# An LSH attention and mixing kernel: a new instruction order, scaling chains in single steps, another bias instruction, and fp32 weights for four heads

## The chip, the cores and the metric

The kernel runs on one core of a Trainium2 chip. The core has four compute engines with a queue of instructions each: PE (TensorE, matmuls; PEld is its weight loads), DVE (VectorE), ACT (ScalarE) and POOL (GpSimd). A fifth queue, SP, issues the DMAs. Each engine works its own queue strictly in order, and waits for other engines by semaphores. The metric is the time of one execution on the device in microseconds (us).

## The reference

Four batches of eight heads, 768 tokens, 64 dimensions a head. Tokens whose six projection signs agree share a bucket and may attend to one another; the heads' outputs, joined to 512 columns, go through a mixing block.

```python
mask = q_bucket[:, :, :, None] == k_bucket[:, :, None, :]
scores = np.where(mask, scale * np.matmul(q, k.transpose(0, 1, 3, 2)), -1e9)
attn = np.exp(scores - np.max(scores, axis=-1, keepdims=True))
attn = attn / (np.sum(attn, axis=-1, keepdims=True) + 1e-09)
x = join_heads(np.matmul(attn, v))
theta = x @ w_theta
y = w_tok_r @ (x * cos(theta)) + w_tok_i @ (x * sin(theta))
u = x + y
out = u + np.maximum(u @ w_ch, 0.0)
```

All inputs are fp32. The kernel reaches that precision with fp16 matmuls on pairs of tiles, a rounded part and the remainder.

## The kernel before

**Staging.** Each operand of a matmul is split into an fp16 high part and an fp16 remainder. The scale for that comes from a sum of squares and a short run of instructions on single columns (128x1): `root_scale` (four of them, for v and for two weight matrices), `pow2_scale` (three, for the six slabs of the token weights) and the seven in `prep_qk` for a pair of heads. In the kernel before each such run is one planned step, so that its instructions stand together in DVE's queue.

**Attention.** For one head, scores come in six chunks of 128x768 in PSUM (`st`). ACT takes the exponential into an fp32 tile `pf`; step p1 (DVE or ACT) rounds it into the first half of an fp16 tile `pp`; step p2 (POOL or DVE) writes the remainder `pf - pp` into the second half; then 18 matmuls, three terms for six blocks, accumulate into `po`. Twenty heads take their row maxima from a second set of scores (`sq`, DVE reduces them into `mx`). Twelve heads of batches 1 to 3 (`turned`, those of TURNED) take the maximum of the chunk itself: DVE reduces PSUM into a column of `bm`, two instructions on that column make a rate and a bias, ACT's exponential waits for both, and `pp` is turned by a DMA into `late` before its matmuls.

**Mixing.** For each batch `moe` makes theta (`ps_th`), `rest` and `mag`, sine and cosine, products `f`, their fp16 parts `z`, the token mix `py` (36 matmuls of 512 columns for 128 rows), and the channel mix `ps_r`. Batch b's mixing lies beside batch b+1's attention; that of the last batch stands alone at the end.

**What sets the order.** A table of text, ORDER, names each step and its engine in one long sequence; `issue_all` walks it and issues each step on the engine named. A second table, SLOTS, gives each step its buffer number. So ORDER decides p1, p2 and the other movable steps' engine and each queue's order; semaphores decide the time. The sequence was made by a planner outside the kernel, which the kernel doesn't hold; the durations in `on(...)` are its figures.

**The switch for single heads.** FULL lists pairs (pair of heads, head in it) of batch 0 that skip p1 and p2: they feed `pf` in fp32 as weights against an fp32 tile `vw` of v. It is empty in the kernel before.

Of the kernel before, what the change touches and what calls it, by code (L numbers as in the profile page):

```python
# [32 lines left out]
def lsh_attention_moe_kernel(ctx: ExitStack, tc: tile.TileContext, q, k, v, proj, w_theta, w_tok_r, w_tok_i, w_ch, aff, out):  # L33
# [133 lines left out]
    sinv, wsum, tinv, tsc = (const.tile([P, T], F32, name=nm) for nm in ("sinv", "wsum", "tinv", "tsc"))  # L167
# [6 lines left out]
    def pow2_scale(amax, inv, s):  # L174
        DVE.tensor_scalar(inv, amax, 1e-30, 2.0**-13, ALU.max, ALU.mult)
        DVE.tensor_scalar(inv.bitcast(U32), inv.bitcast(U32), MASK, None, ALU.bitwise_and)
        DVE.tensor_scalar(s.bitcast(U32), inv.bitcast(U32), MASK, None, ALU.bitwise_xor)

    def root_scale(total, r, inv):
        DVE.tensor_scalar(r, total, 1e-30, None, ALU.max)  # L180
        DVE.tensor_scalar(r.bitcast(U32), r.bitcast(U32), 24, 23, ALU.logical_shift_right, ALU.logical_shift_left)
        DVE.tensor_scalar(inv, r, 2.0**66, None, ALU.mult)
        DVE.tensor_scalar(r.bitcast(U32), inv.bitcast(U32), MASK, None, ALU.bitwise_xor)

    def widened(srcs, n, nm, tag, prio, am=None, stage="x", by=1.0, scaled=None, into=None, hold=()):
# [32 lines left out]
        if scaled:  # L218
            h_ = op("wscale", prio, on("DVE", 440, lambda: scaled(t)), [t["abs"]])
# [10 lines left out]
    def prep_weight(src, dst, nm, n, tag, stage, prio, step, by=1.0):  # L230
# [18 lines left out]
        def joined():  # L249
            DVE.tensor_reduce(col, sums, AX.X, ALU.add)  # L250
            DVE.tensor_scalar(col, col, 2.0**-14, col, ALU.mult, ALU.mult)
            DVE.tensor_scalar(col, col, 2.0**-14, None, ALU.mult)
# [6 lines left out]
        a = op("wcol", last_, on("DVE", 450, joined), done)  # L259
        a = op("wall", last_, on("PE", 60, total), [a], [sa])  # L260
        r = op("wcsc", last_, on("DVE", 620, lambda: root_scale(u["pa"], csc[nm], cinv[nm])), [a], [sa])
# [57 lines left out]
    def prep_v(b, hp, prio):  # L319
# [35 lines left out]
        def scale():  # L355
            root_scale(t["pa"], sc, vinv[:, col])
# [52 lines left out]
        r = op("vscale", prio, on("DVE", 630, scale), [r], [sa])  # L409
# [30 lines left out]
    def prep_qk(b, hp, G, g):  # L440
# [45 lines left out]
        def scale():  # L486
            c = t["sc"]
            sq_, sk_ = c[:, 2:3], c[:, 3:4]
            DVE.tensor_scalar(sk_, t["pa"][:, 0:1], 1e-30, None, ALU.max)
            DVE.reciprocal(sk_, sk_)  # L490
            DVE.tensor_scalar(sq_, t["pa"][:, 1:2], 1e-30, sk_, ALU.max, ALU.mult)
            DVE.tensor_scalar(sq_.bitcast(U32), sq_.bitcast(U32), 24, 23, ALU.logical_shift_right, ALU.logical_shift_left)
            DVE.tensor_scalar(sq_, sq_, 2.0**64 * math.sqrt(UNIT), None, ALU.mult)
            DVE.tensor_scalar(sk_.bitcast(U32), sq_.bitcast(U32), MASK, None, ALU.bitwise_xor)
            DVE.tensor_scalar(sk_, sk_, UNIT / 2, None, ALU.mult)
# [264 lines left out]
    def turned(g, b, h, n_, asm, vt, pieces):  # L760
# [5 lines left out]
        for i in range(T):  # L766
            def one(i=i, before=done[-1:]):
# [22 lines left out]
                def bias():  # L790
                    DVE.scalar_tensor_tensor(part(2), part(0), math.log(PSC) / CEXP, part(1), ALU.add, ALU.mult)  # L791
# [295 lines left out]
FULL = []  # L1087
# [52 lines left out]
D5n D91 A5t P66 P68 D67 D69 A99 A62 P64 S2 D65 P9a P6c D6d P6a D6b P6e D6f A1x P6g A92 S7i S7h P7n A94 P7j D95 A5 D6h S6j D6i D93 D7k P96  # L1140
D7o Scb P6l A1y D9b P6q D3 A6m D6n P7r A6r A9c P6v G6o D7s D63 A6w P70 S6k A71 Scd P7p Pcl D97 S9h P7l S9i A6x G6y P6p D9d D7q D7m Acc P7t
D7u A6s P75 G6t P7v D1z D7w Ace S7y A76 Pcf D7x P7a S7z P9n Dcg P6u A7b A72 A7c D9o P9p D9q P6z A77 P9j G73 Acj D9k P9r D9s Ach Dck P9e P85
# [12 lines left out]
Ahl Ghm Si7 A22 P1l Pju Djv Ajl D33 A35 D23 Pi9 Aia Phd Sl7 D34 Pk4 Si8 Aib Phi Dk5 Dmr Pie Pk0 A36 Gic Aif A1m Pij Phn Dk1 Aig Djm G37 S38
Pjw Dho Gih Djx Aik Ail Amu Pid Dim Pio Dmv D1n Gjn Pit Aip Aiq Pk6 D39 Dk7 Aiu Gjo Dhp Pii Aiv Giw Pin Piy P27 A3b D3a Aiz Sl8 Plf Sk9 Pjp
# [136 lines left out]
```

## Time and profile before

| | before |
|---|---|
| median of three runs | 798.91 us (797.78 to 803.15) |
| the profiled execution | 801.53 us, span of its instructions 799.8 us |
| PE busy | 683.9 us, 86% |
| DVE busy | 690.1 us, 86% |
| ACT busy | 498.6 us, 62% |
| POOL busy | 377.5 us, 47% |

An engine is counted busy while one of its instructions is shown as running. That includes time in which an instruction has started and is held up inside, so a busy share is no measure of work done.

### The profile page before, as it was taken

To read this page: it belongs to the slowest core of one execution; us is meant where nothing else is said; L and a number is where in the kernel's file an instruction comes from. 1 tells how busy PE (TensorE), PEld (TensorE's weight loads), DVE (VectorE), ACT (ScalarE), POOL (GpSimd) and SP (SyncE) were. 2 spreads that over 40 slices of the span, in tenths; PEclk is the share of its full clock that TensorE was granted. 3 is DMA by queue.
4 is the path that set the end of the run, shared out by engine and by line. 5 is a ranking of instruction groups with operands and counts; after the bars stand their busy time and mean duration, and the time that the engine had idled before them with its cause. 6 is when DMAs were issued, how large, how long until landed. Compare 5 with 4: busy or idle time off the path is not lost.

```text
span 799.8 us, 16615 instructions
## 1 busy us (share of the span) xinstructions
PE 683.9 (86%) x6372; PEld 389.3 (49%) x6372; DVE 690.1 (86%) x1210; ACT 498.6 (62%) x702; POOL 377.5 (47%) x258
## 2 busy tenths in 40 slices
PE   3877877878779889898798998899989988979997
PEld 1355655544434455555453564455535454534443
DVE  7979999999999999899999989889998868978412
ACT  6867987976676566766765567548865455545011
POOL 3266767853576544575454445363435234223101
PEclk9988999989999999999989999999999999989999
DMA  6435444433358566697544965996347744862114
GB/s 238 139 91 148 127 131 136 118 127 97 70 141 168 128 136 155 137 165 175 118 85 103 174 129 125 153 203 156 80 113 132 115 97 83 146 124 66 27 40 118
DMA packets 198415, 100.31 MB, mean 125 GB/s; under 512 B 170608, under 2 KB 188096, under 8 KB 198336
## 3 DMA queue, kind: packets, MB, share of 16 engines
q1 hardware_dynamic: 198336, 99.26, 55.6%
q8 instruction: 50, 0.82, 0.4%
q14 instruction: 29, 0.24, 0.1%
HBM read 32.51 MB, written 6.29 MB: 49 GB/s over the span
## 4 chain that ended last, share of the span: by engine, by line
DVE 45%; PE 26%; DMA 9%; ACT 7%; issue 7%; POOL 3%; SPq 2%; DVEq 0%; ACTq 0%; POOLq 0%
PE py L82 8%; DVE mx L610 5%; PE st L82 5%; DVE bm L785 4%; PE po L82 4%; DVE f L974 4%; DVE pp L668 3%; PE ps_r L82 3%; DVE hl L470 3%; DVE bm L791 3%; DMA late<-pp 2%; DVE pp L672 2%; DMA w_t<-in_moe_w_tok_i_dram 2%; PE ps_th L82 2%; POOL pp L672 2%
## 5 line engine op out<-in xcount | busy, mean ns | idle before, releaser
L672 POOL TENSOR_TENSOR pp<-pf,pp 128x768 f16<-128x768 f32 x154 | 280.6, 1831 | 273.0 <-DVE pp L668 115.8
L82 PE MATMUL py<-z,wtk 128*128 128x512 f16 x864 | 210.3, 386 | 11.6 <-POOL z L985 4.8
L655 ACT ACTIVATE pf<-st 128x768 f32<-128x768 f32 x120 | 95.7, 805 | 67.4 <-PE st L82 45.0
L82 PEld LDWEIGHTS <-wtk 128*128 128x128 f16 x864 | 83.9, 99 | 107.4 <-issue 22.7
L610 DVE TENSOR_REDUCE mx<-sq 128x1 f32<-128x768 f32 x120 | 111.9, 948 | 15.3 <-PE sq L82 14.9
L666 ACT ACTIVATE pp<-pf 128x768 f16<-128x768 f32 x131 | 108.9, 838 | 24.5 <-DMA late<-pp 12.6
L657 ACT ACTIVATE pf<-st,bm 128x768 f32<-128x768 f32 x72 | 70.7, 987 | 68.0 <-DVE bm L791 49.2
L82 PE MATMUL st<-qt,kt 108*128 108x384 f16 x480 | 100.7, 337 | 9.7 <-ACT pf L655 3.9
L82 PEld LDWEIGHTS <-pp 128*128 128x128 f16 x2160 | 86.4, 100 | 35.3 <-issue 9.5
L82 PE MATMUL po<-vv,pp 128*128 128x65 f16 (+1 forms) x2160 | 93.3, 197 | 11.6 <-DVE pp L672 5.9
L82 PEld LDWEIGHTS <-qt 108*128 108x128 f16 (+1 forms) x528 | 50.3, 102 | 81.1 <-issue 52.8
L985 POOL TENSOR_TENSOR z<-f,z 128x512 f16<-128x512 f32 x36 | 48.3, 1347 | 86.3 <-ACT z L979 47.0
L82 PE MATMUL sq<-kt,qt 108*128 108x384 f16 x240 | 62.6, 351 | 21.2 <-ACT pf L655 6.9
L82 PE MATMUL ps_th<-wth,t_x 128*128 128x512 f16 x288 | 71.0, 397 | 8.7 <-DMA t_x<-s_x 6.6
L785 DVE TENSOR_REDUCE bm<-st 128x1 f32<-128x768 f32 x72 | 67.8, 947 | 8.3 <-PE st L82 8.3
L82 PE MATMUL st<-kt,qt 108*128 108x384 f16 (+1 forms) x288 | 60.6, 335 | 16.1 <-ACT pf L657 15.1
L82 PE MATMUL ps_r<-wch,t_u 128*128 128x512 f16 x288 | 70.3, 384 | 1.0 <-DMA t_u<-s_u 0.9
L82 PEld LDWEIGHTS <-kt 108*128 108x128 f16 x480 | 45.3, 101 | 44.8 <-issue 21.5
L82 PEld LDWEIGHTS <-late 128*128 128x128 f16 x1296 | 48.1, 99 | 14.6 <-issue 2.8
L82 PE MATMUL po<-vv,late 128*128 128x65 f16 x1296 | 50.3, 195 | 4.5 <-DMA late<-pp 1.9
L668 DVE CAST pp<-pf 128x768 f16<-128x768 f32 x61 | 42.9, 705 | 9.2 <-DMA late<-pp 5.1
L82 PEld LDWEIGHTS <-t_x 128*128 128x128 f16 x288 | 28.2, 102 | 42.9 <-issue 8.3
(166 smaller groups left out, 995.3 us busy)
## 6 DMA issues: line engine op xcount, KB each, us to landing
raw<-in_q_dram SPq DMA_DIRECT2D x16, 384.0 KB
raw<-in_k_dram SPq DMA_DIRECT2D x16, 384.0 KB
vb<-in_v_dram SPq DMA_DIRECT2D x16, 384.0 KB
out_dram<-x SPq DMA_DIRECT2D x24, 256.0 KB
qt<-hl SPq DMA_DIRECT2D x31, 192.0 KB
kt<-hl SPq DMA_DIRECT2D x31, 192.0 KB
w_t<-in_moe_w_tok_r_dram SPq DMA_DIRECT2D x6, 768.0 KB
w_t<-in_moe_w_tok_i_dram SPq DMA_DIRECT2D x6, 768.0 KB
```

The lines of the kernel that those rows point to most:

```text
L82: PE.matmul(out_, l, r, start=start, stop=stop, skip_group_check=True)
L470: DVE.scalar_tensor_tensor(t["hl"][:, 1, i], t["raw", i], t["sc"][:, 2 + i : 3 + i], t["hl"][:, 0, i], ALU.mult, ALU.subtract)
L610: DVE.tensor_reduce(col()[:, i : i + 1], u["sq"], AX.XY, ALU.max)
L655: ACT.activation(u["f"], u["w"], AF.Exp, scale=CEXP)
L657: ACT.activation(u["f"], u["w"], AF.Exp, bias=bias(), scale=scale())
L666: ACT.activation(u["p"][:, 0], flat(), AF.Copy)
L668: DVE.tensor_copy(u["p"][:, 0], flat())
L672: return lambda: eng.tensor_tensor(u["p"][:, 1], flat(), u["p"][:, 0], ALU.subtract)
L785: DVE.tensor_reduce(part(0), u["w"], AX.XY, ALU.max, negate=True)
L791: DVE.scalar_tensor_tensor(part(2), part(0), math.log(PSC) / CEXP, part(1), ALU.add, ALU.mult)
L974: DVE.scalar_tensor_tensor(u["f"], tl[b][:, tt], zsc[:, b : b + 1], t["zw"][r][:, tt], ALU.mult, ALU.mult)
L985: return lambda: eng.tensor_tensor(t["z"][r, 1][:, tt], u["f"], t["z"][r, 0][:, tt], ALU.subtract)
```

## The change

1. **A new ORDER and new SLOTS.** All of both tables. In the new sequence GpSimd's steps and those VectorE steps whose operands lie in SBUF are laid out in turns. Steps also change engine.
2. **Chains.** `root_scale`, `pow2_scale`, the seven instructions of `prep_qk` and three of `prep_weight` become lists; a new `chain` makes each instruction a step of its own, so that ORDER can put other instructions between them.
3. **Bias.** The second column instruction of a turned chunk is `tensor_scalar` where it was `scalar_tensor_tensor`, with the same numbers.
4. **Four heads in fp32.** FULL holds the second head of each pair of batch 0: 24 chunks lose p1, p2 and 18 fp16 matmuls each and gain six fp32 matmuls each.

```diff
+    def chain(name, prio, fns, deps=(), slots=()):
+        r = list(deps)
+        for f in fns:
+            r = [op(name, prio, on("DVE", 75, f), r, slots)]
+        return r[0]
...
     def root_scale(total, r, inv):
-        DVE.tensor_scalar(r, total, 1e-30, None, ALU.max)
-        DVE.tensor_scalar(r.bitcast(U32), r.bitcast(U32), 24, 23, ALU.logical_shift_right, ALU.logical_shift_left)
-        DVE.tensor_scalar(inv, r, 2.0**66, None, ALU.mult)
-        DVE.tensor_scalar(r.bitcast(U32), inv.bitcast(U32), MASK, None, ALU.bitwise_xor)
+        return [
+            lambda: DVE.tensor_scalar(r, total(), 1e-30, None, ALU.max),
...
-        r = op("qksc", pr, on("DVE", 1260, scale), [r], [sa, ssc])
+        r = chain("qksc", pr, scale, [r], [sa, ssc])
...
                 def bias():
-                    DVE.scalar_tensor_tensor(part(2), part(0), math.log(PSC) / CEXP, part(1), ALU.add, ALU.mult)
+                    DVE.tensor_scalar(part(2), part(0), math.log(PSC) / CEXP, part(1), ALU.add, ALU.mult)
...
-FULL = []
+FULL = [(0, 1), (1, 1), (2, 1), (3, 1)]
...
-S5c A5d S5e A5f P5g S0 D1 P5m D5h S5v A5w D5o P5x S1u D5y A5k D5l A5i D5j S8w A5z D60 A5u S8y A5r P61 S98 D1v A5q D5s A8x A8z P90 A5p D1w
+S60 A61 S5y A5z P62 S0 D1 P6e S6n D63 D64 D65 D66 D67 D6g D68 A6o P6p D6q D69 A6a S22 D6f A6c D6d S8d D6r D6b S9h D6s A25 D6i D6k D6h D6l
```

Instructions of the built programs, where their numbers differ:

| instruction | before | after |
|---|---|---|
| PE, fp16 matmuls po from `pp` | 2160 | 1728 |
| PE, fp32 matmuls po from `pf` and `vw` | 0 | 144 |
| PE, fp32 matmuls pm from `vw` | 0 | 24 |
| DVE, casts of `pf` (p1) | 61 | 38 |
| ACT, casts of `pf` (p1) | 131 | 130 |
| POOL, remainders of `pf` (p2) | 154 | 129 |
| DVE, remainders of `pf` (p2) | 38 | 39 |
| POOL, remainders `z` | 36 | 18 |
| DVE, remainders `z` | 12 | 30 |
| DVE, casts to `z` | 27 | 17 |
| ACT, casts to `z` | 21 | 31 |
| DVE, casts of `x` and `u` (`s_x`, `s_u`) | 23 | 18 |
| ACT, casts of `x` and `u` | 25 | 30 |
| POOL, final sums of `x` | 15 | 18 |

DVE's queue, the run of seven for the third pair of heads of batch 1 (`sc_1_2`), before the change; `f` and `z` are products and parts of batch 0's mixing:

```order
L974 SCALAR_TENSOR_TENSOR f_0_1_0_3016<-x_0_656,zsc_111,z1_0_2569 128x512
L981 CAST z1_0_2569<-f_0_0_1_3014 128x512
L489 TENSOR_SCALAR sc_1_2_2780<-pq_1_2_3020 128x1
L490 RECIPROCAL sc_1_2_2780<-sc_1_2_2780 128x1
L491 TENSOR_SCALAR sc_1_2_2780<-pq_1_2_3020,sc_1_2_2780 128x1
L492 TENSOR_SCALAR sc_1_2_2780<-sc_1_2_2780 128x1
L493 TENSOR_SCALAR sc_1_2_2780<-sc_1_2_2780 128x1
L494 TENSOR_SCALAR sc_1_2_2780<-sc_1_2_2780 128x1
L495 TENSOR_SCALAR sc_1_2_2780<-sc_1_2_2780 128x1
L940 SCALAR_TENSOR_TENSOR z1_0_2569<-n_0_4_3055,mg_0_2562,ps_th0_4_2956 128x512
```

The same run in DVE's queue of the change; `bm` are the rate (L803) and bias (L806) of a turned head, `sinv` and `scw` the run of three of a token slab:

```order
L504 RECIPROCAL sc_1_2_2426<-sc_1_2_2426 128x1
L505 TENSOR_SCALAR sc_1_2_2426<-pq_1_2_2749,sc_1_2_2426 128x1
L803 TENSOR_SCALAR bm_1_2_1_2754<-bm_1_2_1_2754 128x1
L182 TENSOR_SCALAR sinv_100<-wsum_101 128x1
L506 TENSOR_SCALAR sc_1_2_2426<-sc_1_2_2426 128x1
L507 TENSOR_SCALAR sc_1_2_2426<-sc_1_2_2426 128x1
L806 TENSOR_SCALAR bm_1_2_1_2754<-bm_1_2_1_2754 128x1
L1000 TENSOR_TENSOR z1_0_2267<-f_0_2_1_2720,z1_0_2267 128x512
L183 TENSOR_SCALAR sinv_100<-sinv_100 128x1
L803 TENSOR_SCALAR bm_1_2_1_2754<-bm_1_2_1_2754 128x1
L806 TENSOR_SCALAR bm_1_2_1_2754<-bm_1_2_1_2754 128x1
L184 TENSOR_SCALAR scw_104<-sinv_100 128x1
```

Three runs now lie in one another, and the bias has become a TENSOR_SCALAR. Over the whole of DVE's queue an instruction of these runs and of the others stands right behind the one whose result it reads 384 times before and 309 times now.

PE's queue at the second chunk of head 1 of batch 0 (`po_0_1_0`), before the change, the first six of 36 rows:

```order
L82 LDWEIGHTS pp_0_1_1_580
L82 MATMUL po_0_1_0_680<-vv0_112,pp_0_1_1_580 128x65
L82 LDWEIGHTS pp_0_1_1_580
L82 MATMUL po_0_1_0_680<-vv0_112,pp_0_1_1_580 128x64
L82 LDWEIGHTS pp_0_1_1_580
L82 MATMUL po_0_1_0_680<-vv0_112,pp_0_1_1_580 128x65
```

The same chunk in PE's queue of the change, with what stands around it (`st` are scores, `pmx` turned row maxima):

```order
L82 LDWEIGHTS kt1_137
L82 MATMUL st_0_1_2_625<-qt1_134,kt1_137 128x384
L82 MATMUL po_0_1_0_605<-vw0_129,pf_0_1_1_578 128x65 x6
L635 MATMUL pmx_0_2_639<-ident_75,mx_0_2_451 6x128
L82 LDWEIGHTS kt1_137
```

Six fp32 matmuls, which load their own weights, stand where 18 pairs stood.

## Rows read from the trace of the kernel before

**Rows 1.** The page: busy us, share of the span and instructions of each engine
```profile
PE 683.9 (86%) x6372; PEld 389.3 (49%) x6372; DVE 690.1 (86%) x1210; ACT 498.6 (62%) x702; POOL 377.5 (47%) x258
```

**Rows 2.** Windows: us, then each engine's busy us and instructions, PEclk, DMA
```profile
50.00:250.00 200.00, 158.84 (x1753) 100.14 (x1752) 191.12 (x309) 157.20 (x236) 133.75 (x74) 0.95 0.45 124
250.00:700.00 450.00, 407.79 (x3962) 234.05 (x3960) 410.82 (x741) 280.13 (x384) 207.05 (x139) 0.97 0.67 133
700.00:800.00 100.00, 86.76 (x479) 40.06 (x477) 48.77 (x77) 27.06 (x36) 19.47 (x14) 0.97 0.32 75
300.00:350.00 50.00, 46.91 (x483) 27.62 (x480) 46.91 (x89) 33.56 (x46) 26.31 (x16) 0.98 0.75 150
```

**Rows 3.** Timeline, DVE, around 400 us: start us, length us, instruction
```profile
400.33 0.15 DVE L788 TENSOR_SCALAR bm<-bm 128x1 f32<-128x1 f32 x1
400.40 0.19 DVE L686 RECIPROCAL rc<-po 128x6 f32<-128x6 f32 x1
400.52 1.58 DVE L791 SCALAR_TENSOR_TENSOR bm<-bm 128x1 f32<-128x1 f32 x1
```

**Rows 4.** Single lines: count, shortest/median/longest ns, first and last start us
```profile
L791 DVE SCALAR_TENSOR_TENSOR bm<-bm x72: 118/160/1644, 222.6 to 702.7; 128x1 f32<-128x1 f32 x72
L788 DVE TENSOR_SCALAR bm<-bm x72: 111/153/155, 221.2 to 702.5; 128x1 f32<-128x1 f32 x72
L859 DVE TENSOR_SCALAR qu<-tinv,zinv,cinv_ch x4: 276/282/1615, 306.5 to 765.4; 128x6 f32<-128x6 f32 x4
L672 POOL TENSOR_TENSOR pp<-pf,pp x154: 1632/1646/4746, 33.3 to 701.4; 128x768 f16<-128x768 f32 x154
L470 DVE SCALAR_TENSOR_TENSOR hl<-raw,sc,hl x32: 996/1012/2481, 11.4 to 645.6; 128x768 f16<-128x768 f32 x32
L974 DVE SCALAR_TENSOR_TENSOR f<-x,zsc,z x48: 735/744/2207, 206.2 to 742.0; 128x512 f32<-128x512 f32 x48
L668 DVE CAST pp<-pf x61: 537/554/1998, 32.6 to 704.2; 128x768 f16<-128x768 f32 x61
L672 DVE TENSOR_TENSOR pp<-pf,pp x38: 939/952/2276, 129.8 to 705.3; 128x768 f16<-128x768 f32 x38
```

**Rows 5.** Groups: line, instruction, count | busy us, mean ns of one | idle before
```profile
L791 DVE SCALAR_TENSOR_TENSOR bm<-bm 128x1 f32<-128x1 f32 x72 | 34.2, 475 | 1.7
L470 DVE SCALAR_TENSOR_TENSOR hl<-raw,sc,hl 128x768 f16<-128x768 f32 x32 | 44.4, 1394 | 0.0
L974 DVE SCALAR_TENSOR_TENSOR f<-x,zsc,z 128x512 f32<-128x512 f32 x48 | 46.6, 986 | 2.0 <-ACT z L963 1.8
L668 DVE CAST pp<-pf 128x768 f16<-128x768 f32 x61 | 42.9, 705 | 9.2 <-DMA late<-pp 5.1 <-ACT pf L657 1.9 <-PE po L82 1.3
L672 DVE TENSOR_TENSOR pp<-pf,pp 128x768 f16<-128x768 f32 x38 | 44.4, 1170 | 3.0 <-ACT pp L666 2.7
```

**Rows 6.** The same view: groups that other terms of the sum use
```profile
L849 DVE TENSOR_SCALAR sw<-sinv,zinv 128x1 f32<-128x1 f32 x6 | 1.2, 200 | 0.0
L985 DVE TENSOR_TENSOR z<-f,z 128x512 f16<-128x512 f32 x12 | 9.8, 825 | 0.1
L981 DVE CAST z<-f 128x512 f16<-128x512 f32 x27 | 14.8, 552 | 0.5
L82 PE MATMUL pa<-vs,ones 128*128 128x1 f32 x32 | 5.6, 243 | 1.2 <-DMA kt<-rows 1.2
```

**Rows 7.** Timeline around 500 us: a run of four for v on DVE
```profile
500.35 0.15 DVE L181 TENSOR_SCALAR vsc<-vsc 128x1 uint32<-128x1 uint32 x1
500.54 0.15 DVE L182 TENSOR_SCALAR vinv<-vsc 128x1 f32<-128x1 f32 x1
```

**Rows 8.** Timeline, PE: an fp16 chunk of po and what follows; four fp32 transposes
```profile
210.44 0.72 PE L82 MATMUL po<-vv,pp 128*128 128x65 f16 x18
211.00 0.33 PE L82 MATMUL st<-qt,kt 108*128 108x384 f16 x1
...
68.71 0.68 PE L290 MATMUL pwt<-ident,wf_t 128*128 128x128 f32 x4
```

More of the change, by code (lines that the diff above doesn't have):

```diff
@@ L166, in lsh_attention_moe_kernel @@
     wtk = {(r, i): wtk_[i][:, r] for r in range(2) for i in range(2)}
-    sinv, wsum, tinv, tsc = (const.tile([P, T], F32, name=nm) for nm in ("sinv", "wsum", "tinv", "tsc"))
+    sinv, wsum, tinv, tsc, scw = (const.tile([P, T], F32, name=nm) for nm in ("sinv", "wsum", "tinv", "tsc", "scw"))
     cinv, csc = {}, {}
@@ L218, in widened @@
         if scaled:
-            h_ = op("wscale", prio, on("DVE", 440, lambda: scaled(t)), [t["abs"]])
+            h_ = chain("wscale", prio, scaled(t), [t["abs"]])
             g = op("wmul", prio, on("DVE", 60 + 535 * k_, lambda: DVE.scalar_tensor_tensor(t["f"], t["f"], t["s"], t["sg"], ALU.mult, ALU.mult)), [d, h_], [sz])
@@ L247, in prep_weight @@
                 done.append(g)
[L249 to L252, printed above, removed]
+        joined = [
+            lambda: DVE.tensor_reduce(col, sums, AX.X, ALU.add),
+            lambda: DVE.tensor_scalar(col, col, 2.0**-14, col, ALU.mult, ALU.mult),
+            lambda: DVE.tensor_scalar(col, col, 2.0**-14, None, ALU.mult),
+        ]
         def total():
@@ L258, in prep_weight @@
         last_ = prio + step * (NC * DM // n - 1)
-        a = op("wcol", last_, on("DVE", 450, joined), done)
+        a = chain("wcol", last_, joined, done)
         a = op("wall", last_, on("PE", 60, total), [a], [sa])
-        r = op("wcsc", last_, on("DVE", 620, lambda: root_scale(u["pa"], csc[nm], cinv[nm])), [a], [sa])
+        r = chain("wcsc", last_, root_scale(lambda: u["pa"], csc[nm], cinv[nm]), [a], [sa])
         for c in range(NC):
@@ L408, in prep_v @@
         r = op("vall", prio, on("PE", 60, total), [r], [svb, sa])
-        r = op("vscale", prio, on("DVE", 630, scale), [r], [sa])
+        r = chain("vscale", prio, scale, [r], [sa])
         vready[b].append(r)
@@ L484, in total, with fq, fk @@
             mm(t["pa"], ones, t["sc"][:, :2], True, True)
[L486 to L495, printed above, removed]
+        def fq():
+            return t["sc"][:, 2:3]
+        def fk():
+            return t["sc"][:, 3:4]
+        scale = [
+            lambda: DVE.tensor_scalar(fk(), t["pa"][:, 0:1], 1e-30, None, ALU.max),
+            lambda: DVE.reciprocal(fk(), fk()),
+            lambda: DVE.tensor_scalar(fq(), t["pa"][:, 1:2], 1e-30, fk(), ALU.max, ALU.mult),
+            lambda: DVE.tensor_scalar(fq().bitcast(U32), fq().bitcast(U32), 24, 23, ALU.logical_shift_right, ALU.logical_shift_left),
+            lambda: DVE.tensor_scalar(fq(), fq(), 2.0**64 * math.sqrt(UNIT), None, ALU.mult),
+            lambda: DVE.tensor_scalar(fk().bitcast(U32), fq().bitcast(U32), MASK, None, ALU.bitwise_xor),
+            lambda: DVE.tensor_scalar(fk(), fk(), UNIT / 2, None, ALU.mult),
+        ]
         r = op("qksum", pr, on("PE", 60, total), sq, [sa, ssc])
-        r = op("qksc", pr, on("DVE", 1260, scale), [r], [sa, ssc])
+        r = chain("qksc", pr, scale, [r], [sa, ssc])
         for i, sn, high, low in parts:
@@ L1137 @@
+    "001111000121130021012020221101310101100020100300110201121"
 )
 ORDER = """
[L1139 to L1142 removed]
@@ L1245 @@
+P2kt A2ku D2kv S2kw
 """
```

251 lines of the change are left out of this document (131 added, 120 removed).

## Prediction

> **What bounds the kernel now.** I read the page's busy times first: DVE and PE are level, 690.1 and 683.9 us of a span of 799.8 [rows 1]. The windows say where each leads. From 50 to 250 us DVE is busy 191.1 of 200 us and PE 158.8; from 250 to 700 us they are level, 410.8 and 407.8 of 450; the last 100 us are the last batch's mixing, PE 86.8 and DVE 48.8 [rows 2]. So DVE leads at first, then both do, then PE.
>
> Then I asked what DVE's busy time is made of. One turned chunk around 400 us shows it [rows 3]: the rate, on one column, takes 0.15 us, and the bias on the same column 1.58. A one-column instruction has no work for 1.58 us; it has started and is held. Over all 72 it takes 160 ns in the median and up to 1644, and GpSimd's remainder takes 1646 in the median [rows 4]: the longest hold is one whole GpSimd instruction. The rate, a TENSOR_SCALAR on the same column, never takes over 155 [rows 4]. Other VectorE work with its operands in SBUF shows the same pair, a short median and a longest about one GpSimd instruction above it: 1012 and 2481 ns for `hl`, 744 and 2207 for `f`, 554 and 1998 for casts of `pf` [rows 4]. So the two engines take turns on something that these forms need.
>
> Mean less median, times the count, is the time held [rows 4, 5]: bias (475 - 160) x 72 = 22.7 us; `hl` (1394 - 1012) x 32 = 12.2; `f` (986 - 744) x 48 = 11.6; casts (705 - 554) x 61 = 9.2; DVE's remainders (1170 - 952) x 38 = 8.3. That is 64.0 us of DVE's 690.1, in five groups alone.
>
> **The bias.** Its nearest row is L849, a TENSOR_SCALAR on one column with a second column as operand: 200 ns in the mean of six [rows 6]. L788, on one column too, speaks for no hold; L859, on six columns with two more operands, for one, 1615 at the longest [rows 4]. Bounds: nothing gained, and 72 x (475 - 153) = 23.2 us. I take L849's mean, since width and kind agree: 72 x (475 - 200) = 19.8 us.
>
> The Trainium skill, "SBUF — State Buffer", section "Who interferes with whom", says that a VectorE instruction with two SBUF inputs shuts out a GpSimd instruction that reads SBUF, and the reverse, and that a `tensor_scalar` can as well, in a mode that uses both ports. The trace agrees on the first (1644 ns against 160). Were the second true of one column, the bias would gain nothing, which is rival 2; rows L788 and L849 speak against it here.
>
> **The turns.** The other four groups are held 41.3 us. How much the new order removes no row shows. From the table itself: behind 78 of GpSimd's 226 entries the next VectorE entry of the old sequence is of a kind held above, and behind 35 of 187 in the new one, a share of 0.35 against 0.19. I let the hold shrink as the counts, 78 to 35, so by 55%: 22.7 us. Bounds: nothing, if the holds only move, and 41.3.
>
> **Moved work on DVE.** Casts of `pf`: 23 fewer at 0.705 = -16.2 us; remainders `z`: 18 more at 0.825 = +14.9; casts to `z`: 10 fewer at 0.552 = -5.5 [rows 5, 6]. One remainder of `pf` more and eight smaller steps handed away about cancel. Net -7 us. ACT takes 15 of the casts, and with 498.6 us busy it has room [rows 1].
>
> **The chains.** A column instruction that reads the one before it starts 0.19 us after it, with a length of 0.15 [rows 7]. One that doesn't starts 0.07 after it (L686 behind L788) [rows 3]. So a neighbour put between saves up to 0.11, and there are 75 fewer such pairs in DVE's queue: 8.3 us. Bounds: nothing and 8.3.
>
> The Trainium skill, "VectorE: DVE Perf Modes", section "The DRAIN you can't avoid", holds that the next operation doesn't start until the pipe is empty, so that only the count of operations matters. By it the chains gain nothing. The trace differs: 400.40 lies inside the 0.15 us that began at 400.33.
>
> **DVE's sum.** 19.8 + 22.7 + 7 + 8.3 = 57.8 us less, 690.1 to 632.3. What covers this gain is PE.
>
> **PE.** An fp16 chunk of 18 pairs takes 0.56 us until the next tile's matmul starts [rows 8]; 24 of them go, 13.4 us. An fp32 matmul leaves two records (the 16 calls for v's sum of squares show 32) [rows 6]. The trace has no fp32 matmul with 128 weight columns and many streamed. Nearest are the transposes, 128x128 fp32: four take 0.68 us [rows 8]; less a last one of about 0.3, which is an estimate from their common length in that row and the 243 ns of the smallest fp32 ones [rows 6], three steps are 0.38, so 0.127 a record. 144 x 2 x 0.127 = 36.6 us. Net +23.2 us, so PE goes to 707. Bounds: records as cheap as fp16 ones (0.56 / 18 = 0.031) give 9.0 - 13.4 = -4.4; records at 0.68 / 4 = 0.17 give 49.0 - 13.4 = +35.6. The 24 for the mean of v are left at nothing: an estimate of 24 x 2 x 0.127 less half of what 48 fp16 ones cost now is under 4 us, and PE is not waited for where they stand, in the first pairs' preparation; without that cover they cost those 4 us.
>
> GpSimd loses 25 remainders and 18 of `z` and so some 55 of its 377.5 us; it bounded nothing, but each of its instructions that goes is one fewer that holds DVE (already in the turns). The fp32 chunks also wait for the exponential alone, no longer for p1 and p2. I price that at nothing: it is cover for PE.
>
> **To time.** I spread DVE's gain over 50 to 700 us, 0.089 us for each. All of PE's cost falls in batch 0, before 250.
> - 50 to 250: DVE 191.1 - 17.8 = 173.3; at its present share of 0.956 that takes 181.3 us. PE 158.8 + 23.2 = 182.0, which doesn't fit. PE becomes the limit. Its best 50 us now are 46.9 of 50, 0.938, with DVE at 46.9 too [rows 2]. With DVE eased I take 0.95: 191.6 us, a gain of 8.4.
> - 250 to 700: DVE 410.8 - 40.0 = 370.8; at its present 0.913 that is 406 us. PE 407.8 / 0.95 = 429.3. A gain of 20.7.
> - the last 100 us: nothing. PE leads there and none of its work goes.
>
> 799.8 - 29.1 = 770.7. The profiled execution lasts 801.53, 1.7 more than its span and 2.6 more than the median, so the median comes to 798.91 - 29.1 = 769.8; I say 770.
>
> **The rivals.**
> 1. *PE packs fully.* PE at 0.98 instead of 0.95 gives 185.7 and 416.1: a gain of 48.2, 751 us. For it: DVE's own sum would allow it, and in batch 0 matmuls no longer wait for p1 and p2. Against: no 50 us stretch in the mixed part shows it.
> 2. *The holds only move.* The bias is held like L859, or the instruction behind it takes its place; the turns remove nothing. Left are 7 + 8.3 = 15.3 us of DVE, over its share of 0.926 from 50 to 700 us (601.9 of 650) 16.5 us: 782. For it: both engines stay one queue each, and an instruction that isn't held may just begin to wait. By the DRAIN rule named above the chains fall out too: 7 us and 791.
> 3. *Slower: the fp32 matmuls lengthen batch 0.* PE stays as loosely packed there as now, 158.8 of 200 or 0.794, because what it waits for is the chain through DVE and DMA and not DVE's total. Then 182.0 / 0.794 = 229 us, a loss of 29; with no gain behind 250 us, 828, with half of the 20.7, 818. It decides where PE's share in that stretch stays under 182.0 / 200 = 0.91 and the rest brings nothing; with the dear record (0.17) that point is at 0.97. For it: PE's share has never been over 0.938. Against: DVE's 0.956 there says who was waited for.
>
> **Chances and range.** The forecast 0.55 (755 to 785), rival 1 0.12, rival 2 0.20, rival 3 0.13. About 1% (8 us) is what a measurement of this kernel can tell from no change, so "faster" is below 791: nearly all of the forecast (0.54), rival 1 (0.12), most of rival 2 (0.15), 0.81. Same: rest of the forecast, of rival 2 and a mild rival 3 (0.01 + 0.05 + 0.03) = 0.09. Slower: 0.10. Range 748 to 797: it leaves out rival 3, 0.13, and some 0.05 of fully packed cases below.
>
> **What the profile of the changed kernel would show.** The bias near 200 ns with a longest near it, not 1600. Mean less median of `hl`, `f`, casts and remainders together near half of 41 us. Chain instructions at 0.15 with neighbours of another tile. fp32 records of po 288 times, starting about 0.127 us apart, PE busy near 707. PE's share in the first 250 us over 0.9. The prediction is wrong if DVE's idle time grows by what its holds lose, if fp32 records cost over 0.17, or if PE's share stays under 0.9 with neither engine full: then it is waiting for DMA or for the order itself.

## The result and the profile after

The changed kernel takes 760.78 us in the median of four executions (759.89 to 761.91), beside 798.75 for the kernel before: a ratio of 0.952, interval 0.948 to 0.955. On a second chip (taken as another one; the first chip's number isn't on record) it took 752.06 us (745.97 to 754.07) beside 798.93, a ratio of 0.941 (0.935 to 0.946). The forecast was 770, range 748 to 797. Executions of some kernels below fall into a faster and a slower group; times and ratios are those of the faster group.

The page of the changed kernel: busy us, share of the span (759.2 us) and instructions of each engine, and the granted clock in 40 slices.

```profile
PE 684.3 (90%) x6276; PEld 404.9 (53%) x6276; DVE 625.3 (82%) x1189; ACT 504.0 (66%) x718; POOL 302.7 (40%) x221
PEclk9899999769999999999999999999999999999999
```

The page on the second chip (span 752.3 us):

```profile
PE 676.9 (90%) x6276; PEld 398.6 (53%) x6276; DVE 624.7 (83%) x1189; ACT 503.8 (67%) x718; POOL 302.4 (40%) x221
```

DVE lost 65 us against [rows 1]; PE is where it was, though some 32 us of fp32 records came (288 at 0.110 us, priced below) and only 13 of fp16 ones went. Its clock explains a part: the mean granted clock was 0.959 before, 0.974 here and 0.983 on the second chip. This isn't one trace's accident: the four executions on the first chip had 0.965 to 0.976, the four on the second 0.983 to 0.990.

Windows of the changed kernel: us, then each engine's busy us and instructions, PEclk, DMA.

```profile
50.00:250.00 200.00, 186.36 (x1687) 130.04 (x1685) 179.24 (x320) 153.13 (x233) 81.89 (x50) 0.92 0.48 129
250.00:700.00 450.00, 414.96 (x4123) 235.53 (x4120) 389.27 (x757) 315.47 (x431) 196.31 (x133) 1.00 0.70 140
130.00:142.00 12.00, 10.06 (x152) 7.09 (x149) 10.79 (x21) 9.34 (x15) 5.13 (x4) 1.00 0.36 98
142.00:166.00 24.00, 24.00 (x107) 19.32 (x106) 13.34 (x28) 9.96 (x18) 5.10 (x5) 0.51 0.15 48
```

The same windows on the second chip:

```profile
50.00:250.00 200.00, 183.34 (x1786) 126.36 (x1785) 190.12 (x350) 160.89 (x247) 91.25 (x58) 1.00 0.53 137
250.00:700.00 450.00, 416.05 (x4063) 234.77 (x4062) 384.42 (x740) 310.89 (x423) 189.00 (x127) 0.99 0.68 136
142.00:166.00 24.00, 22.59 (x218) 17.48 (x217) 21.53 (x47) 19.03 (x32) 9.43 (x8) 1.00 0.36 125
```

The second chip shows the change without that stretch at half clock. From 50 to 250 us DVE is again busy 190 of 200 us, as in [rows 2], and gets 350 instructions done there instead of 309. From 250 us on neither engine is full: PE 416 and DVE 384 of 450. On the first chip PE ran from 142 to 166 us at 0.51, its 1.2 GHz level, and completed 107 matmuls where the second completed 218.

That stretch is nearly all of the difference between the chips' traces. Line L989, the products `f` of the mixing (L974 before), marks the stages by its first and last start. On the first chip:

```profile
L989 DVE SCALAR_TENSOR_TENSOR f<-x,zsc,z x48: 735/748/2132, 197.2 to 701.9; 128x512 f32<-128x512 f32 x48
L806 DVE TENSOR_SCALAR bm<-bm x72: 174/214/215, 211.9 to 666.7; 128x1 f32<-128x1 f32 x72
```

On the second:

```profile
L989 DVE SCALAR_TENSOR_TENSOR f<-x,zsc,z x48: 736/747/2133, 186.8 to 694.9; 128x512 f32<-128x512 f32 x48
```

The first start, 206.2 before [rows 4], comes 9.0 us earlier on the first chip and 19.4 on the second, the span ends 40.6 and 47.5 earlier. So the first chip is 10.4 us behind when batch 0's stretch is over, and later work gives 3.5 of it back. On the second chip 19.4 us of the gain lie before the first product and 28.1 behind it.

The groups of the changed kernel on DVE: line, instruction, count | busy us, mean ns | idle before (L806 is the bias, L480 `hl`, L683 the casts, L687 the remainders).

```profile
L989 DVE SCALAR_TENSOR_TENSOR f<-x,zsc,z 128x512 f32<-128x512 f32 x48 | 45.1, 956 | 2.2 <-ACT z L978 1.5 <-ACT z L977 0.4
L687 DVE TENSOR_TENSOR pp<-pf,pp 128x768 f16<-128x768 f32 x39 | 38.1, 980 | 11.3 <-ACT pp L681 8.2 <-issue 2.1 <-POOL pp L687 0.7
L480 DVE SCALAR_TENSOR_TENSOR hl<-raw,sc,hl 128x768 f16<-128x768 f32 x32 | 35.2, 1111 | 0.1
L683 DVE CAST pp<-pf 128x768 f16<-128x768 f32 x38 | 23.5, 619 | 3.4 <-ACT pf L672 1.1 <-ACT pf L670 0.9 <-PE po L82 0.8
L806 DVE TENSOR_SCALAR bm<-bm 128x1 f32<-128x1 f32 x72 | 15.1, 210 | 1.7
```

Against [rows 5] the bias fell from 475 to 210 ns with no long one left (215 at most), `hl` from 1394 to 1111, remainders from 1170 to 980, casts from 705 to 619; `f` kept most of its hold.

### The profile page after: what moved, and what is told of

Read it like the earlier page. It is cut to its first block, busy times and chain, and to the rows that moved or that the text cites. A ratio compares the mean times of both kernels' runs of the same rounds, so it can differ in the third digit from the quotient of the medians.

```text
span 759.2 us, 16320 instructions
## 1 busy us (share of the span) xinstructions
PE 684.3 (90%) x6276; PEld 404.9 (53%) x6276; DVE 625.3 (82%) x1189; ACT 504.0 (66%) x718; POOL 302.7 (40%) x221
## 5 line engine op out<-in xcount | busy, mean ns | idle before, releaser
L687 POOL TENSOR_TENSOR pp<-pf,pp 128x768 f16<-128x768 f32 x129 | 227.0, 1768 | 303.7 <-ACT pp L681 186.6
L82 PE MATMUL py<-z,wtk 128*128 128x512 f16 x864 | 205.7, 381 | 3.2 <-DVE rows L530 1.2
L82 PE MATMUL sq<-kt,qt 108*128 108x384 f16 x240 | 60.8, 341 | 18.2 <-DVE qt L554 6.9
L82 PE MATMUL ps_th<-wth,t_x 128*128 128x512 f16 x288 | 68.2, 386 | 5.5 <-DMA t_x<-s_x 4.7
L82 PEld LDWEIGHTS <-pp 128*128 128x128 f16 x1728 | 64.7, 98 | 14.1 <-POOL pp L687 3.2
L82 PE MATMUL po<-vv,pp 128*128 128x65 f16 (+1 forms) x1728 | 68.9, 193 | 3.7 <-POOL pp L687 2.9
L82 PE MATMUL st<-kt,qt 108*128 108x384 f16 (+1 forms) x288 | 58.3, 325 | 8.9 <-ACT pf L672 5.4
L82 PEld LDWEIGHTS <-kt 108*128 108x128 f16 x480 | 46.1, 102 | 36.4 <-issue 12.7
L1041 POOL TENSOR_TENSOR x<-rl,x 128x512 f32<-128x512 f32 x18 | 23.9, 1338 | 66.9 <-ACT rl L1038 66.9
L687 DVE TENSOR_TENSOR pp<-pf,pp 128x768 f16<-128x768 f32 x39 | 38.1, 980 | 11.3 <-ACT pp L681 8.2
```

What stands on the lines that cost most here:

```text
L82: PE.matmul(out_, l, r, start=start, stop=stop, skip_group_check=True)
L687: return lambda: eng.tensor_tensor(u["p"][:, 1], flat(), u["p"][:, 0], ALU.subtract)
L1041: return lambda: eng.tensor_tensor(tl[b][:, to], v_["r"], tl[b][:, to], ALU.add)
```

## The experiments

Each run had runs of the kernel before beside it on its chip; ratios are against those. The first four experiments share one chip, the changed kernel's second run and the three with more or less work another, the last four a third. "Hold" is mean less median times count, as in the prediction, with each run's own medians, over `hl`, `f`, casts and remainders: 41.3 us before, 16.6 after.

### The bias alone

```diff
-DVE.scalar_tensor_tensor(part(2), part(0), math.log(PSC) / CEXP, part(1), ALU.add, ALU.mult)
+DVE.tensor_scalar(part(2), part(0), math.log(PSC) / CEXP, part(1), ALU.add, ALU.mult)
```

> The kernel before with one edit: the bias as tensor_scalar. Theory A (a held instruction is lost DVE time, and DVE leads from 200 to 700 us): the bias line falls from 475 ns to about 210, DVE's busy time by 19 us, and at DVE's share of 0.93 the time by 10 to 19 us, to 780-789 us. Rival B (the hold only moves to the next instruction that needs the same thing): the bias line falls, but the holds of hl, f, casts and remainders grow by as much, DVE stays within 5 us of 690 busy, and the time stays within 5 us of the kernel before.

791.1 us, ratio 0.993 (0.990 to 0.995). The page:

```profile
PE 681.1 (86%) x6372; PEld 389.1 (49%) x6372; DVE 680.2 (86%) x1210; ACT 498.1 (63%) x702; POOL 380.5 (48%) x258
```

Two of its groups on DVE, the bias and the parts of v:

```profile
L791 DVE TENSOR_SCALAR bm<-bm 128x1 f32<-128x1 f32 x72 | 15.2, 210 | 1.7
L368 DVE SCALAR_TENSOR_TENSOR vv<-vb,vsc,vv 128x768 f16<-128x768 f32 x16 | 25.6, 1597 | 0.0
```

The instruction lost its hold at once, 72 x (475 - 210) = 19.1 us, but DVE's busy time fell by only 9.9: others were held instead, `vv` alone from 1282 ns to 1597. Its row in the trace of before:

```profile
L368 DVE SCALAR_TENSOR_TENSOR vv<-vb,vsc,vv 128x768 f16<-128x768 f32 x16 | 20.5, 1282 | 0.0
```

In the old order half of the saving moves to neighbours, and 6 us of time remain, between theory A and rival B.

### The change without the bias

```diff
-DVE.tensor_scalar(part(2), part(0), math.log(PSC) / CEXP, part(1), ALU.add, ALU.mult)
+DVE.scalar_tensor_tensor(part(2), part(0), math.log(PSC) / CEXP, part(1), ALU.add, ALU.mult)
```

> The changed kernel with one edit undone: the bias as scalar_tensor_tensor again, in the new order. Theory A (DVE is no longer the limit, PE is): the bias line is held again, 300 to 475 ns, DVE gains 6 to 19 us of busy time, but the time rises by only 2 to 10 us, to 763-771. Theory A' (DVE still limits): the time rises by all that DVE gains, 10 to 19 us. Rival B (holds only move): within 2 us of 760.8.

752.24 us, ratio 0.943 (0.938 to 0.947). The page:

```profile
PE 674.6 (90%) x6276; PEld 396.6 (53%) x6276; DVE 634.9 (85%) x1189; ACT 505.3 (67%) x718; POOL 301.6 (40%) x221
```

The bias among its groups on DVE:

```profile
L806 DVE SCALAR_TENSOR_TENSOR bm<-bm 128x1 f32<-128x1 f32 x72 | 33.6, 467 | 1.7
```

The bias is held again and DVE is 10 us busier, yet the time is that of the full change on the second chip (0.941). So in the new order the new bias instruction is worth nothing that these runs can tell; by the two intervals, up to some 7 us of it could be hidden. Here too about half moves: the bias is held 18.5 us more and DVE is 10.2 us busier.

### The fp32 heads in the old order

The bias of the first experiment, and `FULL` filled; the old ORDER without the p1 and p2 entries of those 24 chunks, ten of their po steps moved ahead:

```diff
-FULL = []
+FULL = [(0, 1), (1, 1), (2, 1), (3, 1)]
```

> The kernel before with the bias as tensor_scalar and the four heads in fp32, its own order kept: the entries of p1 and p2 of these heads are left out, ten of their po chunks stand earlier, since pf has three buffers. Theory A (the gain comes from the holds that the new order avoids and from the bias; fp32 costs PE some 19 us and frees no VectorE time in batch 0, whose casts lay on ACT): not faster than the run with the bias alone by more than 5 us, and up to 10 us slower. Rival F (the shorter way from the exponential to po, and 24 GpSimd instructions fewer in batch 0, are the main gain): 15 us or more faster than the run with the bias alone, near 765-770.

805.24 us (800.6 to 811.43), ratio 1.009 (1.005 to 1.013): 14.1 us slower than with the bias alone, 4 us more than theory A allowed. The page, of the fastest execution:

```profile
PE 702.0 (88%) x6276; PEld 414.0 (52%) x6276; DVE 660.5 (83%) x1205; ACT 483.1 (60%) x684; POOL 334.8 (42%) x239
```

A window of it:

```profile
125.00:150.00 25.00, 25.00 (x115) 21.45 (x116) 8.94 (x20) 9.08 (x15) 3.65 (x3) 0.52 0.27 79
```

Held groups on DVE (`f`, casts, remainders, `hl`):

```profile
L974 DVE SCALAR_TENSOR_TENSOR f<-x,zsc,z 128x512 f32<-128x512 f32 x48 | 46.5, 984 | 2.0 <-ACT z L963 1.8
L668 DVE CAST pp<-pf 128x768 f16<-128x768 f32 x59 | 42.9, 729 | 8.9 <-DMA late<-pp 4.2 <-ACT pf L655 1.7 <-PE po L82 1.5
L672 DVE TENSOR_TENSOR pp<-pf,pp 128x768 f16<-128x768 f32 x35 | 41.8, 1195 | 2.5 <-ACT pp L666 2.2
L470 DVE SCALAR_TENSOR_TENSOR hl<-raw,sc,hl 128x768 f16<-128x768 f32 x32 | 41.5, 1301 | 2.3 <-ACT hl L464 2.3
```

Three things follow. The fp32 heads don't bring the gain by themselves: laid into the old order they cost time, with a stretch of 25 us at half clock in it. DVE's 20 us less buy nothing there. And fewer GpSimd instructions alone do not end the holds: GpSimd lost 46 us of its 380.5, and the four groups are still held 39.3 us. The changed kernel's 16.6 come with the new order: they are 14.7 with the old bias in it (second experiment) and 18.2 with the chains joined (next one).

### The chains joined again

In the new order, each run's instructions put back together at the place of its first, in 42 runs:

```diff
-D65 D66 D67 D6g D68 A6o P6p D6q D69
+D65 D66 D67 D68 D69 D6g A6o P6p D6q D6r D6s D6t
```

> The changed kernel with the instructions of each of the 42 runs on single columns put together again, at the place of the run's first; all else in the new order. Theory A (a dependent neighbour costs 0.11 us, 8 us of DVE in all, and DVE has room now): 0 to 4 us slower, 761-765. Rival G (the single steps are a main gain, since other work no longer stands behind a run of 1.3 us): 8 us or more slower.

755.16 us, ratio 0.947 (0.942 to 0.951). The page:

```profile
PE 680.9 (90%) x6276; PEld 400.9 (53%) x6276; DVE 630.1 (83%) x1189; ACT 503.8 (66%) x718; POOL 302.9 (40%) x221
```

The middle of one run of seven on DVE's timeline:

```profile
116.59 0.15 DVE L506 TENSOR_SCALAR sc<-sc 128x1 uint32<-128x1 uint32 x1
116.78 0.15 DVE L507 TENSOR_SCALAR sc<-sc 128x1 f32<-128x1 f32 x1
116.97 0.15 DVE L508 TENSOR_SCALAR sc<-sc 128x1 uint32<-128x1 uint32 x1
```

The same run on the timeline of the change, second chip:

```profile
117.20 0.15 DVE L506 TENSOR_SCALAR sc<-sc 128x1 uint32<-128x1 uint32 x1
117.27 0.68 DVE L305 TENSOR_TENSOR wtk<-pwt,wtk 128x512 f16<-128x512 f32 x1
117.86 0.14 DVE L507 TENSOR_SCALAR sc<-sc 128x1 f32<-128x1 f32 x1
```

A dependent step starts 0.19 us after the one before it, an unrelated one 0.07. The single steps save 5.4 us of DVE's busy time; the 3 us of time against the second chip's 752.06 lie within the intervals, as theory A had it.

### The changed kernel on a second chip

> The changed kernel once more, on the chip of the next three. Its first trace has one stretch of 23.9 us at half clock (142 to 166 us, while PE is full of fp32 matmuls), and the run with the scalar_tensor_tensor bias has none and is 8 us faster, though nothing of the bias runs before 200 us. Theory C (the clock, not the bias, made that difference): where this run shows such a stretch it takes 758-762 us, where it shows none 750-756. Rival (the bias as scalar_tensor_tensor is itself better in the new order): 758-762 also with no such stretch.

The numbers stand above: with the clock at 0.983 and no such stretch the kernel takes 752.06 us, as theory C has it, 8.7 us less; in the traces it leads by 10.4 us at the first product `f`, behind the half-clock stretch.

### More work on DVE, more work on PE, less work on PE

Three edits of the changed kernel. DVE: each of the 36 norms of a head issued twice, 22 us. PE: one of the two `sq` matmuls issued twice, 120 x 0.165 = 20 us. And the four heads' `pf` and v in fp16 with the same six matmuls a chunk (of that edit only the tile of v is shown).

```diff
+            DVE.scalar_tensor_tensor(dst, t["acc"][:, lo:hi, :D], vt["inv"], t["rc", lo][:, lo:hi].unsqueeze(2).to_broadcast([P, n_, D]), ALU.mult, ALU.mult)
...
+                        if y == 0:
+                            mm(u["sq"][:, y], qt[:K1, 0, ts(i, P)], kt[:K1, 0, y * HS : (y + 1) * HS], True, True)
...
-    vws = [const.tile([P, T, W1], F32, name=f"vw{i}") for i in range(min(len(FULL), 2))]
+    vws = [const.tile([P, T, W1], F16, name=f"vw{i}") for i in range(min(len(FULL), 2))]
```

> The changed kernel with every normalisation out of PSUM (the 36 of line 710) issued twice: 20 us more for DVE, spread over all heads, with no SBUF-only form. Theory A (PE is now the limit, DVE has room): 3 to 9 us slower than the changed kernel. Theory A' (DVE still limits): 15 to 20 us slower.

> The changed kernel with one of the two matmuls of each score tile for the row maxima (sq) issued twice: 120 matmuls of 384 columns at 0.165 us, 20 us more for PE in the twenty heads that are not turned. Theory A (PE is the limit): 10 to 18 us slower than the changed kernel, more than the 20 us on DVE cost. Theory A' (DVE still limits): under 7 us slower.

> The changed kernel, same order, with pf and v of the four heads in fp16 instead of fp32: six fp16 matmuls a chunk. It leaves out the remainders of these 24 chunks, so it is less precise there. It prices fp32. Theory C: PE needs about 288 x 0.112 - 144 x 0.031 = 28 us less in the first 170 us, no stretch of half clock longer than 7 us there, and the eighth head ends 10 to 20 us before 170; the total falls to 740-752. Rival (the stretch comes from how PE waits for DVE and DMA there, fp32 or not): the stretch stays, and the total is within 5 us of the changed kernel.

Beside 752.06 for the change on the same chip: 766.8 with more DVE (0.962, 0.956 to 0.968), 754.74 with more PE (0.945, 0.941 to 0.950), 750.94 with less PE (0.942, 0.936 to 0.948). The page with more DVE:

```profile
PE 681.0 (89%) x6276; PEld 399.0 (52%) x6276; DVE 647.3 (85%) x1225; ACT 505.2 (66%) x718; POOL 298.8 (39%) x221
```

The page with more PE:

```profile
PE 690.4 (92%) x6396; PEld 407.5 (54%) x6396; DVE 622.9 (83%) x1189; ACT 505.3 (67%) x718; POOL 303.4 (40%) x221
```

The page with less PE:

```profile
PE 654.2 (88%) x6108; PEld 369.4 (49%) x6108; DVE 622.7 (83%) x1189; ACT 504.1 (67%) x718; POOL 304.3 (41%) x221
```

DVE's 22.6 us more cost 14.7, clear of the intervals; PE's 13.5 us more in busy time (20 of work) cost 2.7 and PE's 22.7 us less bring 1.1, both inside them. So theory A missed twice and A' came near: added DVE work goes through to the time, and PE, though the busier of the two, has slack where these matmuls stand. With fp16 the time is in theory C's range and in the rival's 5 us as well, the first product comes no earlier (186.6 us against 186.8), and a stretch of half clock of 10 us is still there, from about 144 us on, where C had none over 7: the rival fits better. A caution: the doubled norm stands at a head's end, so part of its price may be that place.

The fp32 step itself was priced a little too high. PE's timeline on the second chip: two fp32 records between fp16 matmuls from `mt`, then a whole chunk and what follows it.

```profile
51.73 0.41 PE L82 MATMUL po<-vw,pf 128*128 128x65 f32 x2
51.98 0.19 PE L82 MATMUL po<-mt,ft 128*128 128x65 f16 x1
52.01 0.41 PE L82 MATMUL po<-vw,pf 128*128 128x65 f32 x2
145.30 1.45 PE L82 MATMUL po<-vw,pf 128*128 128x65 f32 x12
146.59 0.27 PE L635 MATMUL pmx<-ident,mx 128*6 128x128 f32 x1
```

One step beside `mt` is 0.28 us with 0.03 of it for `mt`, so 0.125 a record; the whole chunk takes 1.29 us until the next tile's matmul, 0.107 a record. Over all 288 the mean from start to next start is 0.110, so 32 us.

### GpSimd without reads, in both orders

GpSimd's remainder reads `pf` and `pp` from SBUF. Here it subtracts 32 columns and fills the other 736 with zeros, twice, so that it takes as long and nearly only writes; the remainders beyond column 32 are left out.

```diff
+                eng.tensor_tensor(u["p"][:, 1, :32], flat()[:, :32], u["p"][:, 0, :32], ALU.subtract)
+                for _ in range(2):
+                    eng.memset(u["p"][:, 1, 32:], 0.0)
```

> The kernel before with GpSimd's 154 remainders of pf replaced: the subtraction over the first 32 columns, then two memsets over the other 736, which read nothing, so that GpSimd is busy about as long. It leaves out these remainders beyond column 32. Theory H (the holds are what the old order lost, and the new order avoids): DVE's busy time falls by 50 to 80 us and the time from 798 to 750-770. Rival O (the old order is slower for other reasons): DVE's busy time falls as much, but the time stays over 780.

> The changed kernel with the same replacement of GpSimd's 129 remainders; it leaves out the same part. Theory H: its order avoids most holds, so it gains less than the kernel before does, 5 to 15 us from 752, to 737-747, and the distance between the two orders shrinks from 46 to under 25 us. Rival O: the distance between the two stays over 35 us.

735.61 us in the old order (0.921, 0.918 to 0.925) and 728.0 in the new (0.912, 0.908 to 0.916). The two pages, the old order's first:

```profile
PE 657.7 (90%) x6372; PEld 377.7 (52%) x6372; DVE 619.8 (85%) x1210; ACT 496.7 (68%) x702; POOL 367.2 (50%) x566
PE 666.6 (92%) x6276; PEld 394.6 (55%) x6276; DVE 591.8 (82%) x1189; ACT 502.7 (69%) x718; POOL 293.5 (41%) x479
```

Groups of the old order: GpSimd's two instructions of a chunk, then casts, `hl` and bias on DVE:

```profile
L677 POOL MEMSET pp<- 128x736 f16 x308 | 225.6, 732 | 8.8
L675 POOL TENSOR_TENSOR pp<-pf,pp 128x32 f16<-128x32 f32 x154 | 57.5, 374 | 227.9 <-ACT pp L666 111.5 <-DVE pp L668 98.2 <-DVE bm L795 8.0
L668 DVE CAST pp<-pf 128x768 f16<-128x768 f32 x61 | 40.3, 662 | 10.3 <-DMA late<-pp 5.6 <-PE po L82 1.9 <-ACT pf L657 1.6
L470 DVE SCALAR_TENSOR_TENSOR hl<-raw,sc,hl 128x768 f16<-128x768 f32 x32 | 33.0, 1040 | 0.0
L798 DVE SCALAR_TENSOR_TENSOR bm<-bm 128x1 f32<-128x1 f32 x72 | 16.6, 230 | 1.7
```

A chunk's work on GpSimd takes 374 + 2 x 732 = 1838 ns, where the remainder's mean before was 1831 (280.6 us for 154), so its results come no sooner. Yet the old kernel is 61 us faster, its old bias takes 230 ns and `hl` 1040. What cost this time was the hold, and it came with GpSimd's reads. Without them the two kernels lie 7.6 us apart; with them 46.9. So some 39 us of the change's gain are holds that it avoids. It doesn't avoid nearly all: without the reads it gains another 24 us, where 5 to 15 were expected.

One thing was not separated. PE's clock rose too, to 0.991 from 0.959, and PE was busy 26 us less with the same matmuls. Part of the 61 us may come by that way.

### More work on PE in the old order

The same doubled `sq` matmul as above, in the kernel before.

> The kernel before with one of the two matmuls of each sq tile issued twice: 120 matmuls, 20 us more for PE. In the changed kernel the same addition cost 2.7 us, and 20 us on DVE cost 14.7. Theory D (DVE limits both kernels): 0 to 5 us slower. Rival L (before, DVE and PE were level from 250 us on): 6 to 15 us slower.

804.78 us (801.68 to 806.14), ratio 1.007 (1.003 to 1.011). The 20 us of PE cost 8.0 here and 2.7 in the new order. The 8.0 lie in rival L's range, but the interval, 2.5 to 9.1 us, reaches into theory D's, and the two prices are not told apart by their intervals. Nothing shows PE's work to be dearer after the change than before it, as the prediction's step would have it.

### DVE's steps handed to ACT

In the new order, 50 of DVE's casts and conversions (the parts of `x` and `z`, and `mag`) moved to ACT at their place:

```diff
-A49 S1uu D1v2
+A49 S1uu A1v2
```

> The changed kernel with 50 steps of the mixing moved from DVE to ACT at their places in the order: the 18 casts of x and u, the 17 casts to z and the 15 magnitudes that DVE still had. DVE loses some 8.9 + 7.2 + 10.7 = 27 us, ACT gains some 34 us on 504. Theory D (DVE limits the changed kernel, 0.72 us of time for one of DVE): 10 to 20 us faster than the changed kernel, 732-742. Rival Q (each engine's queue is planned tightly, and a step put into ACT's queue delays the exponentials behind it): no faster than 748, or slower than the changed kernel.

It takes 767.05 and 774.04 us (two executions), 15 and 22 us more than the change on the second chip; theory D missed. The page of the slower of the two:

```profile
PE 683.3 (89%) x6276; PEld 400.1 (52%) x6276; DVE 604.4 (78%) x1139; ACT 533.2 (69%) x768; POOL 299.5 (39%) x221
```

Two rows of its waits (who waits <- for whom: us, times, longest us):

```profile
POOL z L1000 <- ACT z L994: 57.5, 12, 18.5
ACT s_u L906 <- DVE x L1028: 23.6, 6, 7.9
```

The same two in the changed kernel on the second chip:

```profile
POOL z L1000 <- ACT z L994: 22.5, 7, 6.8
ACT s_u L906 <- DVE x L1028: 4.5, 3, 3.4
```

DVE was 20 us less busy and the kernel slower: at the new places ACT waits longer for DVE with its whole queue behind it, and GpSimd for ACT. DVE's total alone doesn't set the time; the order of each queue has to fit the others.

## Why the prediction was right, and where it was not

**What bounds the kernel, and the hold: right, and shown.** A one-column instruction of 1.58 us was read as held, and the other forms' mean above their median as time held. With GpSimd only writing, bias and `hl` lost it. By the Trainium skill, "SBUF — State Buffer", section "Who interferes with whom", it is reading GpSimd instructions that shut out VectorE's two-input forms: the trace agrees (475 to 230 ns for the bias, 1394 to 1040 for `hl`). Casts stay partly held, 662 ns against a median of 556; which of GpSimd's instructions hold them was not tried.

**The bias: its size right, its worth not.** 19.1 us of the predicted 19.8 left the instruction, and a one-column TENSOR_SCALAR is not held. But the first experiment shows half of it moving to neighbours (the first half of rival 2), and the second shows the same half moving in the new order and no worth in time that could be told. The step priced the edit as if it stood alone and added it to the turns; the two overlap.

**The turns: right.** The four groups' hold fell by 24.7 us, predicted 22.7 by counting neighbours in the table. Where it left is uneven: `hl` 8.9, remainders 7.5, casts 6.7, `f` 1.6. Of this, 3.5 us left with the 23 casts that DVE no longer does (23 x 0.151); the prediction counted part of that twice, in the turns and, at 0.705 a cast, in the moved work. The experiment with fp32 heads in the old order shows that GpSimd's lighter load alone doesn't do it.

**Chains: 5.4 us instead of 8.3, and little in time.** The prediction read the Trainium skill, "VectorE: DVE Perf Modes", section "The DRAIN you can't avoid", as leaving them no gain. That section also says that a next operation that is not held starts earlier, and the timeline agrees: L305 starts 0.07 us into an instruction of 0.15.

**DVE's sum: 57.8 predicted, 65.4 measured on the second chip.** The terms named come near: 19.1 + 24.4 + 5.4, and moved work of casts -23 x 0.554 = -12.7, remainders `z` +15.0, casts to `z` -7.7, so 5.4: in all 54.3. The 11 us left lie in groups that the sum had not counted. `vv` lost 4.5 us (20.5 to 16.0 in two shapes) and the remainder of `s_x` 4.4, which are holds. The eight smaller steps handed away, said to about cancel, took some 7.6 us with them (casts of `x` and `u`, final sums); small rises elsewhere take part of that back.

**PE: near a record, wrong in the total.** A record took 0.110 us in the mean (predicted 0.127), 32 us for 288 instead of 36.6. PE's busy time was to reach 707 and is 677 to 684. Busy time is no fixed amount: by the mean clocks, 0.041 x 799.8 us were lost to the low clock before and 0.017 x 752.3 on the second chip, so some 20 us less, an estimate that takes PE as busy whenever the clock was low. The rest of the 30 us is not accounted for.

**"PE becomes the limit": this step failed.** It said that 182.0 us of PE don't fit beside DVE's 173.3 from 50 to 250 us, and that PE at 0.95 sets the time there and behind. On the second chip DVE is at 0.95 in that stretch and PE at 0.92, and behind it PE at 0.92 too; adding or removing 20 us of PE moves the time by 3 or 1 us, adding to DVE by 14.7. On the first chip the same stretch has PE at 0.93 and DVE at 0.90, near the prediction's picture, but there 24 us of half clock filled PE. The prediction let 29.1 of DVE's 57.8 us through to the time, a half. Measured, DVE's idle time grew by only 17.9 us (109.7 to 127.6 on the second chip), so 47.5 of 65.4 came through, 0.73; the added norms give 14.7 / 22.6 = 0.65. This is a ratio of these runs, not a rate to count on: 20 us less of DVE bought nothing with the fp32 heads in the old order, nor with its steps handed to ACT.

That the forecast came out as near as 770 against 760.78 is in part luck: more was saved on DVE, and more of it came through, than forecast, and the first chip's clock stretch took 10 us back. On the second chip it was 18 us off.

**Where the gain lies: half right.** Up to the first product the forecast had some 8 us, and behind it 20.7. The first chip shows 9.0 and 31.6, the second 19.4 and 28.1. From the last product to the end nothing changed, as forecast: 57.8 us before and 57.4 on the second chip.

**The rivals.** PE packing fully (0.98) doesn't occur: 0.92 in both stretches; its time of 751 was reached by another way. Holds that only move occur for half of the bias, in both orders. Fp32 matmuls that lengthen batch 0 occur in the old order: its first product starts at 215.3 us, against 206.9 with the bias alone. On the first chip the half-clock stretch has the same effect. Neither decides.

## What to carry to other kernels

An engine whose one-column instruction takes 1.6 us is being held, and mean less median by group prices it; in a kernel that lays out the two engines' SBUF work in turns, avoided holds are most of the 47 us here, while freeing one instruction alone passed half of its hold to others. Two engines of equal busy time are not two equal limits: ask it of the kernel by adding work to each, since PE at 0.92 took 20 us more for 3. Work taken off the limiting engine helps only where the queue that takes it is not made late by it.

## What the runs showed of the hardware that was not expected

**Half clock while PE is full.** From 142 to 166 us on the first chip PE was busy the whole 24 us, at 0.51, and before it (130 to 142 us) 10.06 of 12 us at 1.00 with no pause over 0.71 us. Its timeline there:

```profile
145.08 2.66 PE L82 MATMUL po<-vw,pf 128*128 128x65 f32 x12
147.53 0.42 PE L635 MATMUL pmx<-ident,mx 128*6 128x128 f32 x1
```

Twelve records take 2.45 us, 0.204 each, where the same chunk takes 1.29 us on the second chip, 0.107 each. The fp32 heads in the old order show such a stretch too, 25 us at 0.52. Seven other traces with fp32 heads show none of this length; the longest is on the second chip, in the 15 us from 30 us on, with PE busy 13.73 us at 0.54. The kernel with fp16 ones had PE busy 8.41 us at 0.50 from 144 to 154 us. Whether the fp32 matmuls bring it about stays open.

**A hold without a price that shows.** The bias held 467 ns in the new order costs 10 us of DVE and no time that could be told; a doubled norm of 22 us costs 14.7. At the norm's price the bias would cost 6 to 7 us, which just fits the intervals, so the two need not differ; more runs of both on one chip would tell. Nor was the new order tried with all heads in rounded parts, so what the fp32 heads are worth inside it, beyond PE's price of about nothing, is open. None of the kernels tried that compute the whole reference beats the change.
